# Turning the normalised rows of two of four batches with transposing DMA transfers instead of TensorE

## The chip, the cores and the metric

One core of a Trainium2 chip runs the whole kernel. The metric is the device time of one execution in microseconds (us); the profiler's span, from the first to the last instruction, is a little shorter. The core has five engines, each with its own in-order instruction stream: PE (TensorE, matrix products; PEld are its weight loads), DVE (VectorE), ACT (ScalarE), POOL (GpSimd) and SP (SyncE, which here only issues DMA transfers). Sixteen DMA engines move the data.

## The reference, cut to what matters

The input is four batches of eight heads with 768 positions of 64 values. First comes a block-sparse causal attention, then a Fourier mixing over positions and features, a normalisation of each row, and an MLP of two matrices with a residual:

```
x   = attention(q, k, v)            # per head: own block and the top 3 of 12 blocks of 64 keys
u   = x + real(fft(fft(x, axis=positions), axis=features))
un  = (u - mean(u)) / sqrt(var(u) + 1e-6)        # per row of 512
out = u + max(un @ w_ch1, 0) @ w_ch2             # 512 -> 2048 -> 512
```

The product `un @ w_ch1` contracts over the 512 features. TensorE contracts over partitions, so `un`, which is computed with positions on the partitions, has to be turned: features onto the partitions.

## The kernel before, in words

All operations of the kernel are first collected as a plan, then put in order by a planner in the kernel (class `Plan`): each operation has a rank, the engines that could do it with a cost on each, the values that it reads and writes, and PSUM banks that it holds. The planner (a list scheduler, `schedule`) starts whatever is ready first, by rank among equals, and its order is written out as the order of instructions on each engine. For a DMA operation it counts an issue cost on SP, a duration on a simulated queue, 1.9 us, and 2.5 us (`LANDING`) until a reader may start. The costs only set the order; on the chip, the engines wait for each other by semaphores.

- `attention(p)` does a pair of heads, 16 pairs in all, four to a batch. Loads of q, k and v come by SP (L367), are cast and split on POOL (casts at the helper's line L688, `klo` L466, `qhl` L461), turned on PE (L478, L527), gated (L542, L581, L585, L594, L606, L616), then scores (PE L639), exponentials (ACT L650), the causal select on the diagonal (POOL L656), the product with v (PE L668, which needs v cast to f16) and the division (DVE L677, L680). The loads of pair p are due well before the pair: their buffers are those of pair p - 2.
- `fourier(b)` does the mixing of batch b after its last pair: sums (L700, L721), two stages of products (PE L739, L743, L773), `u` (DVE L779), row statistics (L786, L789, ACT L797, L801, DVE L805) and the normalised rows, written in place into the tile `x` (`apply`: ACT L813 or DVE L817). A row tile `st` is 128 positions by 512 features, f16; six make a batch. They are done in two halves of three.
- The turn, also in `fourier(b)`: for each row tile, four TensorE transposes of 128 by 128 into one PSUM bank (`un_turn`, L831) and one copy into `unT[:, :, 128*st : 128*st+128]` on DVE (L688) or ACT (L687). There is one `unT` for all batches, [128, 4, 768] f16, so a turn must wait until the last product of the batch before has read the part that it overwrites.
- `mlp(b)` does, for each half (384 positions), 16 up-projections of four matmuls (PE L853, which read `unT` and `w_ch1`), the ReLU (ACT L865 or DVE L867), then three down-projections of 16 matmuls (PE L878), the sum with `u` (DVE L884) and a store of 256 KB to the output (SP, L367). It has a low rank, so its matmuls fill PE between the attention groups of the next batch. The MLP of batch 3, and what is left of batch 2's, run after the attention.

SP's queue thus holds the loads of q, k and v and the stores of the output, in the planner's order.

Of the kernel before, what the change touches and what calls it, by code (L numbers as in the profile page):

```python
# [278 lines left out]
def kernel(  # L279
# [9 lines left out]
    nc = tc.nc  # L289
    B, H, _, D = q.shape  # L290
# [11 lines left out]
    def sb(shape, dtype, name):  # L302
        return cpool.tile(shape, dtype, tag=name, name=name)
# [46 lines left out]
    unT = sb([128, 4, S], F16, "unT")  # L350
# [12 lines left out]
    P = Plan()  # L363
# [10 lines left out]
    def small(rank, e, cost, fn, r=(), w=(), ps=(), pre=(), port=False, rel=0.0):  # L374
        engs = e if isinstance(e, dict) else {e: cost}
        P.op(rank, engs, fn, r=r, w=w, ps=ps, pre=pre, port=port, rel=rel)
# [6 lines left out]
    for i in range(2):  # L383
        small(0.2 + i, "DVE", 0.06,
              lambda x, n, i=i: nc.vector.memset(ind32[64 * i:64 * i + 64, i:i + 1], 1.0),
              r=["ind32"], w=["ind32"])
# [6 lines left out]
    for i in range(NH):  # L393
        small(0, "DVE", 0.07, lambda x, n, i=i: nc.vector.memset(qhl[i][:, :, 0, 64:128], 0.0),
              w=[("qz", i)])
    for i in range(2):
        small(0.5, "DVE", 0.2, lambda x, n, i=i: nc.vector.memset(gmp[i], 0.0), w=[("gmp", i)])
    for i in range(NV):
        small(0.6, "DVE", 0.07, lambda x, n, i=i: nc.vector.memset(V16[i][:, :, :, 64:66], 0.0),
              w=[("vone", i)])  # L400
        small(0.6, "DVE", 0.07, lambda x, n, i=i: nc.vector.memset(V16[i][:, :, :, 64:65], 1.0),
              r=[("vone", i)], w=[("vone", i)])
# [282 lines left out]
    def _copy(x, dst, src):  # L685
        if x == "ACT":
            return nc.scalar.copy(out=dst, in_=src)  # L687
        return eng[x].tensor_copy(out=dst, in_=src)  # L688


    def fourier(b):
        base = 1000 * (HP * b + HP - 1) + (1700 if b == 0 else 500)
        x3, u2 = b % 3, b % 2
        X, U = xb[x3], ub[u2]
        fe = {"DVE": 0.27, "POOL": 0.87}
        for hp in range(HP):
            cols = slice(128 * hp, 128 * hp + 128)
            for r, op in ((0, OP.add), (1, OP.subtract)):
                small(base, fe, 0,
                      lambda x, n, cols=cols, r=r, op=op: eng[x].tensor_tensor(  # L700
                          out=fs[:, r, :, cols], in0=X[:, 0:3, cols], in1=X[:, 3:6, cols], op=op),
                      port=True,
                      r=[("x", x3, 2 * hp), ("x", x3, 2 * hp + 1)], w=[("fs", hp, r)],
# [5 lines left out]
        for i, op in ((0, OP.add), (1, OP.subtract)):  # L709
            small(base + 1, f1, 0,  # L710
                  lambda x, n, i=i, op=op: eng[x].tensor_tensor(
                      out=pm[:, i, :, 1:256], in0=fsf[:, :, 1:256], in1=fsf[:, :, 511:256:-1],
                      op=op),
                  r=allf, w=[("pm", i)], port=True)
        small(base + 1, "ACT", 0.2,
              lambda x, n: nc.scalar.copy(out=pm[:, 0, :, 0:257:256], in_=fsf[:, :, 0:257:256]),
              r=allf, w=["pm0"])
        for i, src, op, lo in ((0, 0, OP.add, 0), (1, 0, OP.subtract, 0),
                               (2, 1, OP.subtract, 0), (3, 1, OP.add, 1)):
            small(base + 2, f2, 0,  # L720
                  lambda x, n, i=i, src=src, op=op, lo=lo: eng[x].tensor_tensor(  # L721
                      out=fk[:, :, i, lo:128], in0=pm[:, src, :, lo:128],
                      in1=pm[:, src, :, 256 - lo:128:-1], op=op),
                  r=[("pm", 0), ("pm", 1), "pm0", "pmz"], w=[("fk", i)], port=True)
        small(base + 2, "ACT", 0.2,
              lambda x, n: nc.scalar.copy(out=fk[:, :, 3, 0:1], in_=pm[:, 1, :, 128:129]),
              r=[("pm", 1)], w=["fk3z"])
        small(base + 2, "ACT", 0.2,
              lambda x, n: nc.scalar.copy(out=xm[:, :, 0:1], in_=pm[:, 0, :, 128:129]),
              r=[("pm", 0)], w=["xm"])  # L730
        for i in range(4):
# [3 lines left out]
            def stage1(x, n, i=i, yp=yp, tab=tab):  # L735
                o = bank32[yp.bank][:, 0:2 * KM].rearrange("p (r m) -> p r m", r=2)
                for r in range(2):
# [3 lines left out]
                    if i == 2:  # L741
# [4 lines left out]
                 r=[("fk", i), "fk3z", "cs", "ss"] + (["xm"] if i == 2 else []),  # L746
                 w=[yp], ps=[yp], pre=[("ty", i), ("trv", i)])
            small(base + 3, {"ACT": 0.46, "DVE": 0.5}, 0,
                  lambda x, n, i=i, yp=yp: _copy(
                      x, ty[i].rearrange("p m r -> p r m"),  # L750
                      bank32[yp.bank][:, 0:2 * KM].rearrange("p (r m) -> p r m", r=2)),
                  r=[yp], w=[("ty", i)], ps=[yp])
            small(base + 3, {"ACT": 0.46, "DVE": 0.5}, 0,
                  lambda x, n, i=i, yp=yp: _copy(
                      x, tr[i].rearrange("p m r -> p r m"),
                      bank32[yp.bank][:, 1:2 * KM - 1]
                      .rearrange("p (r m) -> p r m", r=2)[:, :, ::-1]),
                  r=[yp], w=[("trv", i)], ps=[yp])
# [3 lines left out]
        for kt in range(NST):  # L762
            mp = P.psum("mm")
            late = 0 if kt < 3 else LATE

            def stage2(x, n, kt=kt, mp=mp):
                for par in range(2):
                    o = bank32[mp.bank][:, 256 * par:256 * par + 256]
                    for j in range(2):
# [7 lines left out]
                 w=[mp], ps=[mp], pre=[("u", u2, kt)])  # L777
            small(base + late + 4, "DVE", 0.61,
                  lambda x, n, kt=kt, mp=mp: nc.vector.tensor_tensor(  # L779
                      out=U[:, kt, :].rearrange("p (l r) -> p r l", r=2),  # L780
                      in0=bank32[mp.bank].rearrange("p (r l) -> p r l", r=2),
                      in1=X[:, kt, :].rearrange("p (l r) -> p r l", r=2), op=OP.add),
                  r=[mp] + xall, w=[("u", u2, kt)], ps=[mp])

            small(base + late + 5, "DVE", 0.6,
                  lambda x, n, kt=kt: nc.vector.bn_stats(out=bst[kt], in_=U[:, kt, :]),  # L786
                  r=[("u", u2, kt)], w=[("bst", kt)])
            small(base + late + 5, "DVE", 0.1,
                  lambda x, n, kt=kt: nc.vector.bn_aggr(out=stat[u2][:, kt, :], in_=bst[kt]),  # L789
                  r=[("bst", kt)], w=[("st", u2, kt)])  # L790
        for hf in range(2):
            sl = slice(3 * hf, 3 * hf + 3)
            late = LATE * hf

            vr, rs, nm = lnv[u2][:, sl], rstd[u2][:, sl], nmr[u2][:, sl]
            small(base + late + 6, "ACT", 0.2,
                  lambda x, n, vr=vr, sl=sl: nc.scalar.activation(  # L797
                      out=vr, in_=stat[u2][:, sl, 1], func=AF.Ln, bias=eps),
                  r=[("st", u2, 3 * hf + i) for i in range(3)] + ["eps"], w=[("lnv", u2, hf)])
            small(base + late + 6, "ACT", 0.2,  # L800
                  lambda x, n, vr=vr, rs=rs: nc.scalar.activation(out=rs, in_=vr, func=AF.Exp,  # L801
                                                                  scale=-0.5),
                  r=[("lnv", u2, hf)], w=[("rs", u2, hf)])
            small(base + late + 6, "DVE", 0.1,
                  lambda x, n, sl=sl, rs=rs, nm=nm: nc.vector.scalar_tensor_tensor(  # L805
                      out=nm, in0=stat[u2][:, sl, 0], scalar=-1.0, in1=rs, op0=OP.mult,
                      op1=OP.mult),
                  r=[("rs", u2, hf)] + [("st", u2, 3 * hf + i) for i in range(3)],
                  w=[("nm", u2, hf)], port=True)
            for st in range(3 * hf, 3 * hf + 3):  # L810
                def apply(x, n, st=st):
                    if x == "ACT":
                        return nc.scalar.activation(out=X[:, st, :], in_=U[:, st, :],  # L813
                                                    func=AF.Identity,
                                                    scale=rstd[u2][:, st:st + 1],
                                                    bias=nmr[u2][:, st:st + 1])
                    return nc.vector.tensor_scalar(out=X[:, st, :], in0=U[:, st, :],  # L817
                                                   scalar1=stat[u2][:, st, 0:1],
                                                   scalar2=rstd[u2][:, st:st + 1],
                                                   op0=OP.subtract, op1=OP.mult)  # L820
                small(base + late + 6, {"DVE": 0.47, "ACT": 0.6}, 0, apply,
                      r=[("u", u2, st), ("rs", u2, hf), ("nm", u2, hf)],
                      w=[("x", x3, h) for h in range(H)] if st == NST - 1 else [("un", x3, st)],
                      port=True)
                if st == NST - 1:
                    P.last_w[("un", x3, st)] = len(P.ops) - 1
                tp = P.psum("tr")

                def un_turn(x, n, st=st, tp=tp):
                    for dt in range(4):  # L830
                        nc.tensor.transpose(bank16[tp.bank][:, 128 * dt:128 * dt + 128],  # L831
                                            X[:, st, 128 * dt:128 * dt + 128], id16)
                P.op(base + late + 7, {"PE": 0.25}, un_turn, r=["sm", ("un", x3, st)], w=[tp], ps=[tp],
                     pre=[("unT", st)])
                small(base + late + 7, {"DVE": 0.34, "ACT": 0.52}, 0,
                      lambda x, n, st=st, tp=tp: _copy(
                          x, unT[:, :, 128 * st:128 * st + 128],
                          bank16[tp.bank][:, 0:512].rearrange("p (a c) -> p a c", a=4)),
                      r=[tp], w=[("unT", st)], ps=[tp])
# [50 lines left out]
    for p in range(NPAIR):  # L890
# [17 lines left out]
        if p > HP and p % HP == 1:  # L908
            fourier(p // HP - 1)
            mlp(p // HP - 1)  # L910
    fourier(B - 1)
    mlp(B - 1)

# [38 lines left out]
```

## Time and profile before

| what | us |
|---|---|
| median of three runs (313.51 to 314.13) | 313.94 |
| the profiled execution | 313.72 |
| its span | 311.5 |
| PE busy / DVE / ACT / POOL | 301.3 / 195.3 / 189.1 / 130.3 |

In the page and the answers of the trace, L12 is line 12 of the kernel. A row of groups has: line, engine, operation, output<-inputs, shapes, count, then busy time in us and the mean of one in ns, then the idle time of the engine just before, with what ended it. A row of the order of time has: start in us, length in us, engine, line, operation, output<-inputs, count, and in brackets the idle time before it. SPq is SP's queue of DMA issues; the time of such a row is the time that the issue held SP. A row of waits has: who waited, for whom, us in total, times, the longest. A matmul's length is that of one in a pipelined array: several are in flight at once.

### The profile page before, as it was taken

How to read it: one execution, taken by the hardware profiler on the slowest of the kernel's cores; microseconds unless marked ns; L12 is line 12 of the kernel's file. 1: busy time of each engine (PE TensorE's matmuls, PEld its weight loads, DVE VectorE, ACT ScalarE, POOL GpSimd, SP SyncE). 2: the span in 40 equal slices, each digit the busy share in tenths (PEclk: the TensorE clock that was granted, in tenths of full speed). 3: DMA queues.
4: the chain of work that ended last, by engine and by line, in shares of the span. 5: the costliest groups of instructions: out<-in, count | busy, mean ns of one | idle time of the engine just before them, and what ended most of it. 6: DMA issues, size and time to landing. Idle time of an engine off the chain costs nothing.

```text
span 311.5 us, 8060 instructions
## 1 busy us (share of the span) xinstructions
PE 301.3 (97%) x3097; PEld 198.5 (64%) x3097; DVE 195.3 (63%) x652; ACT 189.1 (61%) x418; POOL 130.3 (42%) x251
## 2 busy tenths in 40 slices
PE   7999999999999999999999999999999999999994
PEld 4767676766647776666666876757655865554641
DVE  4797989997655899755548797856425694002001
ACT  2579898779508788478644699708661671540710
POOL 4258897836546181748273453837025000000000
PEclk9999999999999999999999999999999999999999
DMA  8999999990066351009320760010001001101001
GB/s 218 257 241 238 246 232 217 228 189 22 0 153 176 81 121 32 36 37 237 78 61 34 187 154 1 36 36 35 2 36 67 2 1 67 37 0 67 36 34 67
DMA packets 82085, 31.12 MB, mean 100 GB/s; under 512 B 75272, under 2 KB 77492, under 8 KB 82048
## 3 DMA queue, kind: packets, MB, share of 16 engines
q1 hardware_dynamic: 77584, 25.77, 33.7%
q0 software_dynamic: 3536, 4.56, 8.1%
q8 instruction: 24, 0.39, 0.5%
q10 hardware_dynamic: 928, 0.30, 0.4%
q14 instruction: 13, 0.11, 0.1%
HBM read 28.52 MB, written 6.29 MB: 112 GB/s over the span
## 4 chain that ended last, share of the span: by engine, by line
PE 80%; DVE 9%; ACT 6%; issue 1%; DMA 1%; SPq 0%; DVEq 0%; ACTq 0%
PE bank L878 27%; PE bank L853 26%; PE bank L639 9%; PE bank L668 5%; ACT pt L650 4%; PE bank L527 3%; PE bank L739 2%; DVE u L779 2%; PE bank L773 2%; PE bank L478 2%; PE bank L831 1%; DMA kn<-in_k_dram 1%; DVE bst L786 1%; DVE qg L616 1%; PE bank L492 1%
## 5 line engine op out<-in xcount | busy, mean ns | idle before, releaser
L650 ACT ACTIVATE pt<-bank 128x512 f16<-128x512 f32 x192 | 88.3, 579 | 23.4 <-PE bank L639 21.7
L853 PE MATMUL bank<-unT,w 128*128 128x384 f16 x512 | 90.7, 326 | 0.2 <-DVE unT L688 0.2
L878 PE MATMUL bank<-w,hT 128*128 128x512 f16 x384 | 89.1, 379 | 0.0
L865 ACT ACTIVATE hT<-bank 128x384 f16<-128x384 f32 x115 | 56.3, 497 | 46.4 <-PE bank L853 45.6
L853 PEld LDWEIGHTS <-w 128*128 128x128 f16 x512 | 48.2, 98 | 30.0 <-issue 0.8
L878 PEld LDWEIGHTS <-hT 128*128 128x128 f16 x384 | 36.0, 98 | 37.6
L639 PE MATMUL bank<-qg,ki 76*128 76x128 f16 (+3 forms) x384 | 51.2, 259 | 0.7 <-ACT pt L650 0.4
L884 DVE TENSOR_TENSOR u<-bank,u 128x512 f32<-128x512 f32 x24 | 16.5, 688 | 51.1 <-PE bank L878 51.0
L639 PEld LDWEIGHTS <-ki 76*128 76x128 f16 x384 | 29.2, 97 | 10.6 <-issue 0.6
L656 POOL TENSOR_SCALAR_AFFINE_SELECT pt<-pt 128x512 f16<-128x512 f16 (+1 forms) x44 | 22.0, 522 | 25.3 <-ACT pt L650 20.6
L668 PEld LDWEIGHTS <-pt 128*128 128x128 f16 x672 | 23.8, 97 | 6.5 <-ACT pt L650 3.0
L668 PE MATMUL bank<-v,pt 128*128 128x65 f16 x672 | 25.6, 193 | 0.6 <-ACT pt L650 0.3
L616 DVE TENSOR_SCALAR qg<-bank 12x384 f16<-12x384 f16 x64 | 20.6, 322 | 7.6 <-PE bank L606 5.7
L466 POOL TENSOR_TENSOR klo<-kn,k 128x384 f16<-128x384 f32 x24 | 21.9, 913 | 5.3 <-DVE rcp L677 1.9
L461 POOL TENSOR_TENSOR qhl<-qn,qhl 128x320 f16<-128x320 f32 x26 | 20.6, 792 | 6.2 <-DVE qhl L688 4.8
L688 POOL CAST k<-kn 128x384 f16<-128x384 f32 x24 | 12.2, 507 | 19.2 <-DVE fs L721 9.0
L688 DVE COPY ki<-bank 64x768 f16<-64x768 f16 x23 | 12.7, 554 | 9.6 <-PE bank L478 7.0
L680 DVE TENSOR_TENSOR x<-bank,rcp 128x384 f16<-128x384 f32 x32 | 17.8, 555 | 0.6
L677 DVE RECIPROCAL rcp<-bank 128x6 f32<-128x6 f32 x32 | 6.2, 193 | 18.0 <-PE bank L668 10.6
L527 PE MATMUL bank<-sm,qhl 128*128 128x128 f16 x192 | 17.1, 229 | 0.1
L779 DVE TENSOR_TENSOR u<-bank,x 128x512 f32<-128x512 f32 x24 | 15.3, 681 | 1.9 <-PE bank L773 1.9
L594 POOL MEMSET gmp<- 64x5 f16 x40 | 4.6, 114 | 27.9 <-DVE gmp L585 26.8
(106 smaller groups left out, 405.6 us busy)
## 6 DMA issues: line engine op xcount, KB each, us to landing
out_dram<-u SPq DMA_DIRECT2D x24, 256.0 KB, 2.0
kn<-in_k_dram SPq DMA_DIRECT2D x28, 192.0 KB, 3.4
vn<-in_v_dram SPq DMA_DIRECT2D x28, 192.0 KB, 3.8
qn<-in_q_dram SPq DMA_DIRECT2D x26, 192.0 KB, 4.4
w<-in_moe_w_ch_dram POOLq DMA_DIRECT2D x16, 256.0 KB, 6.7
hT<-in_k_dram SPq DMA_DIRECT2D x4, 192.0 KB, 4.3
hT<-in_q_dram SPq DMA_DIRECT2D x4, 192.0 KB, 4.2
hT<-in_v_dram SPq DMA_DIRECT2D x4, 192.0 KB, 3.7
```

The lines of the kernel that those rows point to most:

```text
L466: lambda x, n, kh=kh, kl=kl, e=e: eng[x].tensor_tensor(out=kl, in0=kn[a][:, :, e, :], in1=kh, op=OP.subtract),
L527: nc.tensor.transpose(bank16[tq.bank][:, 128 * st:128 * st + 128], qhl[h2][:, e, st, :], id16)
L616: nc.vector.tensor_scalar(out=rows[:, i::2, :], in0=turned[at:at + NB, 0:3 - i, :], scalar1=-NEG, scalar2=NEG, op0=OP.mult, op1=OP.add)
L639: nc.tensor.matmul(bank32[sp.bank][:, co:co + a1 - a0], KI[e][g3][0:76, 128 * jt:128 * jt + 128], QG[e][g3][0:76, a0:a1], start=not added, ...
L650: lambda x, n, sp=sp, pt=pt, at=at, wid=wid: nc.scalar.activation(out=pt[:, at:at + wid], in_=bank32[sp.bank][:, 0:wid], func=AF.Exp, scal ...
L656: lambda x, n, pt=pt, at=at, nd=nd: nc.gpsimd.affine_select(out=pt[:, at:at + 128 * nd].rearrange("p (a c) -> p a c", a=nd), in_=pt[:, at: ...
L668: nc.tensor.matmul(o[:, st, 0:65], pt[:, col:col + 128], V16[v4][:, e, jt, 0:65], start=(i == 0), stop=(i == 20))
L688: return eng[x].tensor_copy(out=dst, in_=src)
L779: lambda x, n, kt=kt, mp=mp: nc.vector.tensor_tensor(out=U[:, kt, :].rearrange("p (l r) -> p r l", r=2), in0=bank32[mp.bank].rearrange("p ...
L853: nc.tensor.matmul(bank32[hp_.bank][:, 0:384], w1[:, dt, 128 * it:128 * it + 128], unT[:, dt, 384 * hf:384 * hf + 384], start=(dt == 0), s ...
L865: nc.scalar.activation(out=o, in_=i_, func=AF.Relu)
L878: nc.tensor.matmul(bank32[cp.bank], hT[hf][:, it, 128 * j:128 * j + 128], w2[:, it, :], start=(it == 0), stop=(it == NIT - 1))
```

## The change

In `fourier(b)`, for batches 1 and 2, the turn becomes one transposing DMA transfer for each row tile, issued from SP, which reads the f16 rows from `x` and writes `unT` directly; there is no PSUM bank, no transpose on PE and no copy. In the plan it costs SP 0.6 and the queue 1.0. Batches 0 and 3 keep the turn on PE.

```diff
                 if st == NST - 1:
                     P.last_w[("un", x3, st)] = len(P.ops) - 1
+                if 0 < b < B - 1:
+                    P.op(base + late + 7, {"SP": 0.6},
+                         lambda x, n, st=st: nc.sync.dma_start_transpose(
+                             out=unT[:, :, 128 * st:128 * st + 128], in_=X[:, st, :]),
+                         r=[("un", x3, st)], w=[("unT", st)], dma=1.0)
+                    continue
                 tp = P.psum("tr")
```

The planner makes a new order from it. Up to the first turn of batch 1 the order of PE's instructions is the same; from there on it differs in places. On SP, the three transfers of batch 1's first half stand ahead of the loads of pair 11, those of batch 2's first half ahead of the loads of pair 15 (the last pairs of batches 2 and 3); the three of each second half stand among stores of the output. Lines behind the inserted ones move by 6: L831 becomes L837, L853 L859, L878 L884.

## The prediction

> **What bounds the kernel now.** I began with the page: busy times, the chain of work that ended last, the DMA queues.
>
> ```profile
> span 311.5 us, 8060 instructions
> PE 301.3 (97%) x3097; PEld 198.5 (64%) x3097; DVE 195.3 (63%) x652; ACT 189.1 (61%) x418; POOL 130.3 (42%) x251
> PE 80%; DVE 9%; ACT 6%; issue 1%; DMA 1%; SPq 0%; DVEq 0%; ACTq 0%
> q1 hardware_dynamic: 77584, 25.77, 33.7%
> out_dram<-u SPq DMA_DIRECT2D x24, 256.0 KB, 2.0
> vn<-in_v_dram SPq DMA_DIRECT2D x28, 192.0 KB, 3.8
> ```
>
> TensorE is busy for 97% of the span and makes up 80% of the chain. But that is an average, so I cut the span into stages (time, busy time by engine, granted clock, DMA share, GB/s) and asked what PE waited for from 80 to 300 us.
>
> ```profile
> 80.00:220.00 140.00, 139.21 (x1522) 94.29 (x1520) 98.59 (x323) 90.20 (x199) 71.44 (x149) 1.00 0.33 83
> 220.00:300.00 80.00, 80.00 (x527) 46.25 (x525) 28.48 (x72) 38.38 (x82) 6.43 (x10) 1.00 0.08 30
> PE bank L639 <- ACT pt L650: 0.4, 1, 0.4
> PE bank L773 <- ACT pt L650: 0.3, 1, 0.3
> 188.44 0.38 PE L639 MATMUL bank<-qg,ki 76*128 76x128 f16 x3 [0.44 <-ACT pt L650]
> ```
>
> From 80 to 220 us, where batches 1 and 2 are turned, PE stands idle for 140.00 - 139.21 = 0.79 us; from 220 to 300 us not at all. DVE, ACT and POOL are busy for 98.59, 90.20 and 71.44 of 140 us and hold PE up only in the two short waits on ACT. The granted clock is 1.00. So from 80 us to the end the time is the sum of PE's work: an instruction taken from PE shortens the run by the time it holds PE, as long as nothing that PE then reads comes late. Work taken from DVE or ACT shortens nothing by itself.
>
> **What the change removes.** A turn of one row tile is four TensorE transposes (L831) and one copy out of PSUM (L687 on ACT or L688 on DVE). The change leaves batches 0 and 3 alone and takes 2 x 6 turns: 48 of the 96 transposes. Busy time overlaps in the pipelined array, so I take the step from the first transpose of a group to the next work in PE's order of time.
>
> ```profile
> L831 PE MATMUL bank<-sm,x x96: 216/219/230, 65.9 to 259.6; 128*128 128x128 f16 x96
> 126.36 0.83 PE L831 MATMUL bank<-sm,x 128*128 128x128 f16 x12
> 127.03 1.03 PE L878 MATMUL bank<-w,hT 128*128 128x512 f16 x4
> 194.93 0.61 PE L831 MATMUL bank<-sm,x 128*128 128x128 f16 x8
> 195.37 1.03 PE L878 MATMUL bank<-w,hT 128*128 128x512 f16 x4
> L688 DVE COPY unT<-bank 128x512 f16<-128x512 f16 x16 | 6.3, 418 | 0.6 <-PE bank L831 0.4
> L687 ACT COPY unT<-bank 128x512 f16<-128x512 f16 x8 | 4.7, 582 | 5.1 <-PE bank L831 5.0
> ```
>
> One transpose is listed with 219 ns, but twelve hold PE for 127.03 - 126.36 = 0.67 us and eight for 195.37 - 194.93 = 0.44 us: 55.5 ns each. So 48 x 55.5 ns = 2.66 us leave PE, all of it in the stage where PE has no gaps. The weight loads go with the transposes and are inside that step. The 12 copies (418 or 582 ns, 5 to 7 us together) leave engines that are not the bound; I cost them at nothing. At best, the two waits on ACT shrink with them, and then at most 0.79 us more is gained.
>
> **What it adds.** Twelve transposing transfers on SP, SBUF to SBUF, 128 KB each. The trace of before has no such transfer, so its duration must be bounded. I call t the time by which one of them pushes back whatever is behind it on SP's queue, by holding the sequencer or by filling the rings. Nearest rows, the SP queue (start, time held) around the first turns of batches 1 and 2:
>
> ```profile
> 111.79 0.37 SPq L367 DMA_DIRECT2D kn<-in_k_dram  x1
> 112.21 0.54 SPq L367 DMA_DIRECT2D qn<-in_q_dram  x1
> 114.42 1.13 SPq L367 DMA_DIRECT2D vn<-in_v_dram  x2
> 126.89 0.36 SPq L367 DMA_DIRECT2D out_dram<-u  x1
> 182.40 1.23 SPq L367 DMA_DIRECT2D vn<-in_v_dram  x2
> ```
>
> A plain store of twice the bytes holds SP for 0.36 us and has landed after 2.0 us; that is the lower end. For the upper end: the compiled instruction moves blocks of 16 rows by 128 columns, so a destination partition receives runs of 16 values, 32 bytes, and a transfer has 128 x 4 x 8 = 4096 such runs. Queue q1 spent 33.7% of 16 engines x 311.5 us on 77584 packets, 21.6 ns a packet. If each run cost as much, a transfer would take 4096 / 16 x 21.6 ns = 5.5 us. Between 0.36 and 5.5 us I take about 1 us, near the load rows (0.54 and 1.13 / 2 = 0.57 us) with something added for the smaller blocks.
>
> The Trainium skill has a rule for each end. DMA: Bandwidth & Descriptors, section Latency and other measured facts, gives a transposing DMA 261 GB/s; as an estimate that is 0.5 us of moving for 128 KB, and the sum stays 311.1. The same page, section Specifications, says that transfers under 512 B are not at line rate because the engine reads, modifies and writes; were the 32-byte runs handled so, the estimate would go to the upper end, and the sum to the slower rival below. No run here shows either.
>
> **Does PE wait for the turned rows?** In batch 1, a transfer can start when its normalised rows are written and the last up-projections of batch 0 have read the old ones; in batch 2, when the rows are written.
>
> ```profile
> 118.48 2.11 PE L853 MATMUL bank<-unT,w 128*128 128x384 f16 x12
> 119.33 0.81 ACT L813 ACTIVATE x<-u,nmr,rstd 128x512 f16<-128x512 f32 x1 [0.19 <-DVE nmr L805]
> 120.22 0.54 DVE L817 TENSOR_SCALAR x<-u,stat,rstd 128x512 f16<-128x512 f32 x1
> 120.20 0.80 ACT L813 ACTIVATE x<-u,nmr,rstd 128x512 f16<-128x512 f32 x1
> 185.69 2.21 ACT L813 ACTIVATE x<-u,nmr,rstd 128x512 f16<-128x512 f32 x3
> 134.85 0.20 PE L514 MATMUL bank<-ka,sm 128*128 128x24 f16 x2
> 137.80 0.81 PE L853 MATMUL bank<-unT,w 128*128 128x384 f16 x4
> 169.66 1.46 PE L853 MATMUL bank<-unT,w 128*128 128x384 f16 x8
> 203.95 0.20 PE L514 MATMUL bank<-ka,sm 128*128 128x24 f16 x2
> ```
>
> The first three transfers of batch 1 start at about 118.48 + 2.11 = 120.6 us, and the third has landed at 120.6 + 3t + 2.0 = 122.6 + 3t. Before, the first up-projection ran at 137.80; in the changed program's order it stands right behind the group that is at 134.85 here. With t = 1 the rows are there at 125.6, 9 us early; PE would wait only from t = 4.1. In batch 2 the first three start at 186.5 (a third of the 2.21 us after 185.69), and the first reader stands behind the group that is at 203.95 here. The second half of batch 1, turned from 126.36 on, is not read before 169.66. So the longer way from rows to rows turned costs nothing; that cover is gone only with t above 4.
>
> **What is queued behind them.** SP works in order. In the changed order the three transfers stand ahead of the loads k, q, k, q, v of pair 11 (batch 1) and of pair 15 (batch 2); before, SP ran ahead and had issued these by 114.42 + 1.13 = 115.6 and by 182.40 + 1.23 = 183.6. Now they leave after the transfers. The second half of v stands also behind an output store, which waits for DVE, and transfers four to six stand among stores. Who is hurt first is POOL, which casts v in order:
>
> ```profile
> 130.05 0.91 POOL L466 TENSOR_TENSOR klo<-kn,k 128x384 f16<-128x384 f32 x1
> 132.47 0.99 POOL L656 TENSOR_SCALAR_AFFINE_SELECT pt<-pt 128x512 f16<-128x512 f16 x2 [1.51 <-ACT pt L650]
> 133.41 0.95 POOL L688 CAST v<-vn 128x384 f16<-128x384 f32 x2
> 201.64 0.95 POOL L688 CAST v<-vn 128x384 f16<-128x384 f32 x2
> ```
>
> In batch 1 the changed order puts the first cast of v before the two selects, right behind klo, so at 130.96. The load of v is issued at 120.6 + 3t + 2.0 (four loads of 0.37 to 0.54 us with their gaps) and lands 3.8 us later, at 126.4 + 3t: 129.4 with t = 1, in time. POOL waits from t = 1.5; PE only when the selects are late, which have 1.51 us of idle time before them, so from t = 2.0. In batch 2 v lands at 186.5 + 3t + 2.0 + 3.8 = 192.3 + 3t and is wanted at about 201: from t = 2.9. With t = 1 both are hidden.
>
> **Sum.** The profiled execution took 313.72 us, 2.2 us more than its span. 313.72 - 2.66 + 0 = 311.06, so 311.1. The median of the three runs, 313.94, lies 0.2 above the profiled one; I work from the latter and leave the 0.2 to the range.
>
> **Rivals.**
> Loads pushed back (slower). Price for PE: in batch 1, 3t - 6.1 above t = 2.0 (132.5 is where the selects run, less 126.4); in batch 2, 3t - 8.7 above t = 2.9. The first alone eats the gain of 2.66 at t = 2.9, so slower begins there. At t = 4 it is 5.9 + 3.3 - 2.66 = 6.5 us, 320.3; at the upper bound of 5.5 us, 10.4 + 7.8 - 2.66 = 15.5 us, 329.3. For it: the 32-byte runs, and the cast of v that moved ahead of the selects. Against it: POOL is idle for half of this stage, and DMA is busy for 0.33 of it.
>
> Gain partly eaten: t between 2.0 and 2.9, or one wait of about 1.5 us where the new order no longer has a transpose to put between attention's groups while ACT is late: 313.72 - 2.66 + 1.5 = 312.6. For it: the 0.44 us wait on ACT at 188.44 stands right beside the turns of batch 2. Against it: ACT loses copies in the same stretch. Up to a loss of 2 to 3 us this ends within 0.2%.
>
> More gain: the 0.79 us of gaps closes too, 313.72 - 2.66 - 0.79 = 310.3. For it: DVE and ACT lose 5 to 7 us. Against it: the order fills these gaps only by chance.
>
> That the transposes of batches 1 and 2 remain can be left out: the compiled program has 48 fewer.
>
> **How the numbers follow.** Forecast 311.1 (310.6 to 311.9): 0.64. More gain, 310.3: 0.06. Partly eaten, 312.6: 0.16, of which 0.06 end within 0.2% (0.6 us, about what a measurement of this kernel can tell from no change: 313.1 to 314.3). Slower, 314.4 to 329: 0.14. So faster is 0.64 + 0.06 + 0.10 = 0.80, same 0.06, slower 0.14. The range 310.2 to 313.4 leaves out the slower rival and little else; t's upper end has its weight there and is beyond the range.
>
> **What would show it.** Right: 48 fewer transposes on PE, PE still at 139 of 140 us in the stage, the same work from 220 us on some 2.7 us earlier, transposing transfers on SP that hold it for about 1 us and have landed some 10 us before the first L853 of their batch (859 in the changed file). Wrong: a wait of POOL's cast of v on a DMA near 131 us, PE waiting for a select or for an attention group behind it, loads landing in much more than 3.8 us beside the transfers, or PE's gaps between 115 and 205 us growing past 0.79 us. The prediction is wrong outright if t is above 2.9 us, or if PE takes up the removed 2.66 us in waits on ACT.

## The result and the profile after

Over 20 runs of each, the changed kernel takes a median of 311.6 us (310.04 to 315.5) and the kernel before 314.05 us (313.19 to 317.55). The ratio is 0.9922, 95% interval [0.99, 0.9943]: 2.45 us faster (1.8 to 3.1).

The execution of the changed kernel that was profiled is not a typical one: 314.68 us, with a span of 313.0. Its page, and the row of its DMA issues for the transfers (count, median us to landing):

```profile
span 313.0 us, 7986 instructions
PE 300.1 (96%) x3049; PEld 197.3 (63%) x3049; DVE 193.8 (62%) x646; ACT 187.1 (60%) x414; POOL 127.7 (41%) x249
PE 74%; DVE 8%; DMA 6%; ACT 4%; SPq 3%; POOL 2%; issue 2%; DVEq 0%; POOLq 0%
q1 hardware_dynamic: 84112, 27.34, 36.6%
```

```profile
unT<-x SPq DMA_TRANSPOSE x12, 2.5
```

PE has 48 matmuls fewer, as it should, yet the span is longer and DMA has come into the chain. The order of time shows where:

```profile
49.42 1.12 POOL L688 CAST qhl<-qn 128x384 f16<-128x384 f32 x1 [2.69 <-DMA qn<-in_q_dram]
```

```profile
55.91 0.45 PE L527 MATMUL bank<-sm,qhl 128*128 128x128 f16 x5 [1.83 <-POOL qhl L461]
```

At 49 us POOL waits 2.69 us for a load of q, and PE 1.83 us behind it. That is about 70 us before the first instruction that the change touches: the start, whose instructions are the same in both kernels, scatters from execution to execution by several us (in this one the granted clock up to the first up-projection was 0.98 against 1.00, and PE stood idle for 7.83 us against 5.38), so traces are compared here from a mark behind it. I took the stretch from the first up-projection (L853, after the change L859) to the first down-projection after the last up-projection. Rows of the view by stages (stretch, its length, busy time and instructions of PE, PEld, DVE, ACT, POOL, clock, DMA share, GB/s), for the kernel before, for the changed one, and for a second profile of the changed one (experiment 10):

```profile
67.35:296.90 229.55, 228.76 (x2162) 147.84 (x2163) 137.69 (x429) 138.55 (x304) 85.38 (x175) 1.00 0.24 64
```

```profile
71.10:298.65 227.55, 226.34 (x2114) 145.28 (x2115) 135.56 (x423) 136.28 (x300) 81.36 (x173) 1.00 0.28 69
```

```profile
70.30:297.85 227.55, 226.34 (x2114) 145.25 (x2115) 135.58 (x423) 136.38 (x300) 81.53 (x173) 1.00 0.30 72
```

The mark stands at 67.35 us in one execution and at 71.10 in the other; from there on, the changed kernel needs 227.55 us instead of 229.55, and it repeats to 0.01 us. So the change is worth 2.00 us in this stretch (2.42 of PE's busy time less, 229.55 - 228.76 = 0.79 us of gaps become 227.55 - 226.34 = 1.21). The tail behind it is 14.60 us before and 14.35 after, but 14.35 to 14.57 in the other runs, with and without the change.

That leaves a part of the 2.45 us. A run lasts a little longer than its span, and this remainder is not the same in both kernels: 313.72 - 311.5 = 2.2 us before, 314.68 - 313.0 = 1.7 us after. It repeats: the medians over the runs are 2.2 to 2.3 us for the kernel before, 1.7 us for the changed one, 1.7 to 1.9 us for every version below with transposing transfers and 2.05 to 2.3 us for every version without. So of the 2.45 us, 2.00 come from the stretch and, by these medians, about 0.5 us from outside the span, where no instruction of the program is; what the scattering start adds or takes cannot be told from one trace each. No experiment was made on that part, and its cause stays open.

PE's waits in the changed kernel from 80 us on, and where the longest stands:

```profile
PE bank L639 <- DVE qg L616: 0.6, 1, 0.6
PE bank L773 <- ACT pt L650: 0.3, 1, 0.3
PE bank L639 <- DVE u L779: 0.2, 1, 0.2
```

```profile
189.25 0.60 PE L639 MATMUL bank<-qg,ki 76*128 76x128 f16 x4 [0.63 <-DVE qg L616]
190.05 0.38 PE L639 MATMUL bank<-qg,ki 76*128 76x512 f16 x1 [0.16 <-DVE u L779]
```

The wait of 0.44 us on ACT at 188.44 is gone; two waits on DVE, 0.79 us together, stand near its place. None is on a transfer. The transfers themselves, on SP's queue, with the summary of their line:

```profile
123.91 3.91 SPq L829 DMA_TRANSPOSE unT<-x  x3
127.91 0.54 SPq L367 DMA_DIRECT2D kn<-in_k_dram  x1
130.26 0.53 SPq L367 DMA_DIRECT2D vn<-in_v_dram  x1
190.94 4.49 SPq L829 DMA_TRANSPOSE unT<-x  x3
195.52 0.53 SPq L367 DMA_DIRECT2D kn<-in_k_dram  x1
```

```profile
L829 SPq DMA_TRANSPOSE unT<-x x12: 1195/1220/1900, 123.9 to 202.8; - x12
DMA to landing us min/median/max: 2.4/2.5/4.2
```

One transfer holds SP for 1.22 us in the median and has landed 2.5 us after its issue. Three of them push the loads back by 127.91 - 123.91 = 4.0 us in batch 1 and by 195.52 - 190.94 = 4.6 us in batch 2, so t is 1.3 and 1.5 us. What stood behind them came just in time:

```profile
133.96 0.92 POOL L466 TENSOR_TENSOR klo<-kn,k 128x384 f16<-128x384 f32 x1
134.82 0.50 POOL L688 CAST v<-vn 128x384 f16<-128x384 f32 x1
136.60 0.99 POOL L656 TENSOR_SCALAR_AFFINE_SELECT pt<-pt 128x512 f16<-128x512 f16 x2 [1.27 <-ACT pt L650]
```

```profile
139.03 0.81 PE L859 MATMUL bank<-unT,w 128*128 128x384 f16 x4
```

The cast of v follows `klo` without a wait, the select still waits for ACT, not for POOL, and the first up-projection comes at 139.03, some 10 us after the third transfer has landed (issued by 126.7, plus 2.5).

### The profile page after: what moved, and what is told of

Read it like the earlier page. It is cut to its first block, busy times and chain, and to the rows that moved or that the text cites. A ratio compares the mean times of both kernels' runs of the same rounds, so it can differ in the third digit from the quotient of the medians.

```text
span 313.0 us, 7986 instructions
## 1 busy us (share of the span) xinstructions
PE 300.1 (96%) x3049; PEld 197.3 (63%) x3049; DVE 193.8 (62%) x646; ACT 187.1 (60%) x414; POOL 127.7 (41%) x249
## 3 DMA queue, kind: packets, MB, share of 16 engines
q1 hardware_dynamic: 84112, 27.34, 36.6%
## 4 chain that ended last, share of the span: by engine, by line
PE 74%; DVE 8%; DMA 6%; ACT 4%; SPq 3%; POOL 2%; issue 2%; DVEq 0%; POOLq 0%
PE bank L884 27%; PE bank L859 26%; PE bank L639 7%; DMA qn<-in_q_dram 5%; PE bank L668 4%; SPq L367 3%; ACT pt L650 3%; PE bank L739 3%; DVE u L779 3%; PE bank L527 2%; DVE bst L786 2%; PE bank L773 1%; DMA vn<-in_v_dram 1%; PE bank L478 1%; PE bank L743 1%
## 5 line engine op out<-in xcount | busy, mean ns | idle before, releaser
L859 PE MATMUL bank<-unT,w 128*128 128x384 f16 x512 | 90.4, 326 | 0.2 <-DVE unT L688 0.2
L884 PE MATMUL bank<-w,hT 128*128 128x512 f16 x384 | 88.7, 379 | 0.0
L871 ACT ACTIVATE hT<-bank 128x384 f16<-128x384 f32 x118 | 57.7, 495 | 42.6 <-PE bank L859 40.5
L859 PEld LDWEIGHTS <-w 128*128 128x128 f16 x512 | 48.2, 98 | 30.1 <-issue 0.9
L884 PEld LDWEIGHTS <-hT 128*128 128x128 f16 x384 | 36.1, 98 | 38.1
L639 PE MATMUL bank<-qg,ki 76*128 76x128 f16 (+3 forms) x384 | 51.1, 259 | 0.9 <-DVE qg L616 0.6
L639 PEld LDWEIGHTS <-ki 76*128 76x128 f16 x384 | 29.2, 97 | 11.1 <-issue 0.9
L668 PEld LDWEIGHTS <-pt 128*128 128x128 f16 x672 | 23.8, 97 | 5.6 <-ACT pt L650 2.3
L668 PE MATMUL bank<-v,pt 128*128 128x65 f16 x672 | 25.6, 193 | 0.2
L461 POOL TENSOR_TENSOR qhl<-qn,qhl 128x320 f16<-128x320 f32 x26 | 21.3, 819 | 6.6 <-DVE qhl L688 5.2
L688 DVE COPY qg<-bank 128x768 f16<-128x768 f16 x24 | 13.2, 551 | 5.1 <-PE bank L527 3.3
```

The lines of the kernel that those rows point to most:

```text
L461: lambda x, n, hi=hi, lo=lo, e=e: eng[x].tensor_tensor(out=lo, in0=qn[a][:, e, 1:NST], in1=hi[:, 1:NST], op=OP.subtract),
L639: nc.tensor.matmul(bank32[sp.bank][:, co:co + a1 - a0], KI[e][g3][0:76, 128 * jt:128 * jt + 128], QG[e][g3][0:76, a0:a1], start=not added, ...
L668: nc.tensor.matmul(o[:, st, 0:65], pt[:, col:col + 128], V16[v4][:, e, jt, 0:65], start=(i == 0), stop=(i == 20))
L859: nc.tensor.matmul(bank32[hp_.bank][:, 0:384], w1[:, dt, 128 * it:128 * it + 128], unT[:, dt, 384 * hf:384 * hf + 384], start=(dt == 0), s ...
L871: nc.scalar.activation(out=o, in_=i_, func=AF.Relu)
L884: nc.tensor.matmul(bank32[cp.bank], hT[hf][:, it, 128 * j:128 * j + 128], w2[:, it, :], start=(it == 0), stop=(it == NIT - 1))
```

## The experiments

Theory A: the gain is PE's time, 48 transposes of 55.5 ns; copies and transfers count for nothing. Rivals: the copies (C), transfers that hold back the loads (B), and, as results came in, waits that the transposes had been covering, and the planner's new order. Each is judged by the row of the stretch defined above; where a ratio is given, it is the ratio of run times to the kernel before, on the same chip. The ratios hold the start and the time outside the span as well, so they do not measure the stretch (experiment 3's says 3.7 us where the stretch says 2.1). Diffs are against the changed kernel, where nothing else is said, and lines that only declare an unused tile are left out of them.

**1. The transfers left out, everything else in the same order.**

```diff
-                         lambda x, n, st=st: nc.sync.dma_start_transpose(
-                             out=unT[:, :, 128 * st:128 * st + 128], in_=X[:, st, :]),
+                         lambda x, n: None,
```

> The changed kernel with the twelve transposing transfers left out and every other instruction in the same order (batches 1 and 2 then multiply rows left in unT by batch 0, so its output is not the reference's). Theory A (PE's time is what was gained, the transfers are hidden): within 0.4 us of the changed kernel's 311.6. Rival B (the transfers hold back loads behind them and cost part of the gain): faster than the changed kernel by the cost, 0.5 to 1.2 us, since PE's gaps of about 1.2 us from 80 us on could go.

```profile
69.91:297.47 227.56, 226.35 (x2114) 145.29 (x2115) 135.62 (x423) 136.26 (x300) 81.36 (x173) 1.00 0.24 63
```

227.56 us with no transfer at all, 227.55 with twelve: they cost nothing in the stretch. Ratio 0.9915 [0.9881, 0.995]. B falls. The run's median, 312.38 us, is not within the expected 0.4 us of 311.6; 0.35 us of this is time outside the span (2.05 us here, 1.70 in the changed kernel), and none of it is in the stretch.

**2. The transposes put back, their result unused.**

```diff
+                    tp = P.psum("tr")
+
+                    def again(x, n, st=st, tp=tp):
+                        for dt in range(4):
+                            nc.tensor.transpose(bank16[tp.bank][:, 128 * dt:128 * dt + 128],
+                                                X[:, st, 128 * dt:128 * dt + 128], id16)
+                    P.op(base + late + 7, {"PE": 0.25}, again, r=["sm", ("un", x3, st)],
+                         w=[tp], ps=[tp])
                     continue
```

> The changed kernel with the 48 TensorE transposes put back, their result unused; the transfers still do the turning and the 12 copies stay away. Theory A (48 x 55.5 ns = 2.66 us of PE are the whole gain): the gain is gone, 314.0 to 314.4, ratio to before 1.000 +- 0.002. Rival C (the relief of DVE and ACT by 12 copies, or fewer waits for a copy): stays near 311.6, ratio 0.992.

```profile
67.01:295.95 228.94, 228.59 (x2162) 147.78 (x2163) 137.36 (x426) 136.86 (x298) 80.40 (x172) 1.00 0.30 73
```

PE's busy time comes back (228.59), but the stretch is 228.94, not 229.55; ratio 0.9937 [0.9901, 0.9974]. PE's gaps are only 0.35 us here. Neither theory had that: 0.61 us of gain is there with all the transposes in place. What else differs from the kernel before is the copies, the transfers, and the planner's order. Experiments 1 and 8 exclude the first two. The order is one of its own: apart from the transposes, PE's matmuls stand neither as in the kernel before nor as in the changed kernel.

**3. Copies added to the changed kernel**, 12 of 128 x 512 on DVE (8) and ACT (4), from SBUF to an unused tile.

```diff
+                    small(base + late + 7, {"DVE": 0.34, "ACT": 0.52}, 0,
+                          lambda x, n, st=st: _copy(
+                              x, idle[:, :, 128 * (st % 3):128 * (st % 3) + 128],
+                              U[:, st, :].rearrange("p (a c) -> p a c", a=4)),
+                          r=[("u", u2, st), ("un", x3, st)], w=[("idle", st % 3)])
```

> The changed kernel with 12 copies of 128 x 512 values added on DVE or ACT (from u in SBUF to an unused tile; those out of PSUM cannot be kept without the transposes); no transposes on PE. Theory A: within 0.4 us of 311.6, ratio 0.992, as DVE and ACT have room. Rival C (copies were the gain): back toward 314, ratio 1.000.

```profile
66.34:293.81 227.47, 226.26 (x2115) 145.26 (x2116) 137.18 (x430) 139.36 (x305) 82.70 (x173) 1.00 0.29 72
```

DVE and ACT are 1.6 and 3.1 us busier than in the changed kernel, the stretch is the same. Ratio 0.9881 [0.983, 0.9932]. Here too the planner moved some of PE's matmuls, so this is copies and a slightly different order together; experiment 8 is the one that leaves the order alone.

**8. The kernel before in its own order, the copies of batches 1 and 2 left out.**

Against the kernel before:

```diff
-                      lambda x, n, st=st, tp=tp: _copy(
+                      lambda x, n, st=st, tp=tp: None if 0 < b < B - 1 else _copy(
```

> The kernel before, its order of instructions unchanged, with the 12 copies out of PSUM of batches 1 and 2 left out (its output is not the reference's): transposes stay on PE. Theory A: 229.5 +- 0.3 us from the first up-projection to the first down-projection after the last, as before, where the changed kernel has 227.6. Rival C (the copies' relief is part of the gain): down to 228.5 or less.

```profile
70.22:299.76 229.54, 228.75 (x2162) 147.77 (x2163) 135.30 (x421) 136.30 (x300) 85.31 (x175) 1.00 0.24 63
```

229.54 against 229.55. Ratio 0.9992 [0.9958, 1.0025]. C falls: with the transposes in place, the copies are worth nothing.

**9. The kernel before in its own order, the 48 transposes left out, the copies kept.**

Against the kernel before (shown in part; the 12 copies now go from the same banks to an unused tile, `idle`):

```diff
-                    for dt in range(4):
+                    for dt in range(0 if 0 < b < B - 1 else 4):
```

> The kernel before, its order of instructions unchanged, with the 48 TensorE transposes of batches 1 and 2 left out and the 12 copies kept (as 16-bit integers from the same banks into an unused tile; batches 1 and 2 then multiply rows left by batch 0, so its output is not the reference's). Theory A (48 x 55.5 ns = 2.66 us of PE, gaps as before): 229.55 - 2.66 = 226.9 us +- 0.15 from the first up-projection to the first down-projection after the last. Rival I (a transpose between other matmuls holds PE for less than the step of a group; the changed kernel lost 2.42 us of busy time, 50 ns each): 227.1 to 227.2. Rival C (the copies): 229.5.

```profile
67.64:295.75 228.11, 226.76 (x2115) 145.18 (x2116) 137.36 (x429) 138.30 (x304) 85.55 (x175) 1.00 0.25 65
```

A miss for every theory: 228.11, only 1.44 us less than before. Ratio 0.9976 [0.9941, 1.0011]. As the order is the same, the two traces can be laid beside each other. The table gives starts on PE, and e9 less before, less the 0.29 us by which e9's mark is later (67.64 - 67.35):

| PE, what starts | before | e9 | ahead by |
|---|---|---|---|
| attention (L668) behind 8 removed transposes | 121.74 | 121.57 | 0.46 |
| k turned (L478) behind 16 more | 127.89 | 126.82 | 1.36 |
| masks turned (L606) | 129.42 | 128.62 | 1.09 |
| scores (L639) behind 8 more | 188.44 | 187.65 | 1.08 |
| scores (L639) behind 4 and 8 more | 196.24 | 194.93 | 1.60 |
| down-projection (L878) behind 4 more | 198.51 | 197.04 | 1.76 |
| attention (L668) | 200.03 | 198.88 | 1.44 |

In batch 1 the 24 transposes give 1.36 us, their full 24 x 55.5 ns = 1.33. Then part of it is given back, at the larger places before an instruction that needs another engine: 0.27 us at the turn of the masks, 0.45 us at the scores at 188 (8 transposes gone, nothing gained), 0.21 us in smaller pieces up to 198 (16 gone, 0.68 us gained instead of 0.89), 0.32 us from there to 200: 1.25 us in all, and 2.66 + 0.03 - 1.25 = 1.44. Two such places in experiment 9:

```profile
128.02 0.50 PE L529 MATMUL bank<-sm,qhl 128*128 128x128 f16 x6
128.62 0.34 PE L608 MATMUL bank<-sm,gmp 128*128 128x128 f16 x3
187.65 0.38 PE L641 MATMUL bank<-qg,ki 76*128 76x128 f16 x3 [0.89 <-ACT pt L652]
126.98 0.74 DVE L690 COPY idle<-bank 128x512 int16<-128x512 int16 x2
127.64 0.29 DVE L587 TENSOR_TENSOR gmp<-gsb,mx 128x120 f16<-128x120 f32 x1
127.99 0.57 POOL L596 MEMSET gmp<- 64x5 f16 x4 [0.20 <-DVE gmp L587]
```

The wait on ACT at 188 is 0.89 us instead of 0.44: the transposes had covered half of it. At 128 there is no wait in brackets, yet six transposes that step 55.5 ns each end their steps at 128.35 and the next matmul starts at 128.62. Of these 0.27 us, 0.17 hide under the listed length of the last matmul in flight (128.02 + 0.50 = 128.52) and count as busy; the other 0.10 is idle time too short for the view's brackets. The next matmul reads the masks `gmp`, which POOL has finished at 127.99 + 0.57 = 128.56, behind DVE. And right before that step of DVE stand two of the kept copies, 0.74 us. The changed kernel has no such copies, so up to 0.27 us of what experiment 9 gives back may be theirs; a run of the old order without transposes and without copies was not made.

**4. Every transfer issued twice, the first into an unused tile.**

```diff
-                         lambda x, n, st=st: nc.sync.dma_start_transpose(
-                             out=unT[:, :, 128 * st:128 * st + 128], in_=X[:, st, :]),
+                         lambda x, n, st=st: [nc.sync.dma_start_transpose(
+                             out=o[:, :, 128 * i:128 * i + 128], in_=X[:, st, :])
+                             for o, i in ((idle, st % 3), (unT, st))][-1],
```

> Each of the twelve transfers issued twice, the first into an unused tile. SP is then held for 2.4 us a row tile instead of 1.2. Theory A with the prediction's own price for loads pushed back (3t - 6.1 in batch 1 above t = 2.0, nothing in batch 2): 3 x 2.44 - 6.1 = 1.2 us lost, 312.8, ratio 0.996. Rival D (POOL's delay never reaches PE): 311.6, ratio 0.992. Rival E (PE pays all of the push, 3 x 1.22 us for each of two batches): 318.9, ratio 1.016.

```profile
66.77:294.33 227.56, 226.35 (x2114) 145.25 (x2115) 135.60 (x423) 136.26 (x300) 81.56 (x173) 1.00 0.33 79
```

```profile
134.04 0.50 POOL L689 CAST v<-vn 128x384 f16<-128x384 f32 x1 [3.48 <-DMA vn<-in_v_dram]
119.58 1.30 SPq L830 DMA_TRANSPOSE idle<-x  x1
127.51 0.53 SPq L368 DMA_DIRECT2D kn<-in_k_dram  x1
```

POOL now waits 3.48 us for v, and PE no longer than in the changed kernel: 227.56. Ratio 0.9877 [0.9829, 0.9925]. Rival D is right; the prediction's price, 1.2 us by the expected t of 2.44, is wrong here. By this trace t was (127.51 - 119.58) / 3 = 2.6, for which the price would be 1.8 us.

**5. Every transfer issued four times**, three into an unused tile. Against experiment 4:

```diff
-                             for o, i in ((idle, st % 3), (unT, st))][-1],
+                             for o, i in ((idle, 0), (idle, 1), (idle, 2), (unT, st))][-1],
```

> Each of the twelve transfers issued four times, three into an unused tile: SP is held for some 4.9 us a row tile. The prediction's price, 3t - 6.1 in batch 1 and 3t - 8.7 in batch 2, gives 8.6 + 6.0 = 14.6 us lost, 326, ratio 1.039. Rival F (with double transfers POOL waited 3.5 us for v and PE not at all, so PE has more slack behind the selects than the prediction counted, about 3 us more in each batch): 6 to 10 us lost, 318 to 322, with PE waiting behind POOL's selects or casts.

```profile
69.72:311.85 242.13, 229.60 (x2115) 146.61 (x2116) 135.75 (x423) 136.61 (x300) 81.67 (x173) 0.98 0.38 86
```

```profile
PE bank L669 <- POOL pt L657: 4.7, 1, 4.7
PE bank L607 <- POOL gmp L595: 4.1, 2, 2.5
PE bank L861 <- DMA unT<-x: 2.6, 1, 2.6
122.53 3.92 SPq L830 DMA_TRANSPOSE idle<-x  x3
139.11 0.58 SPq L368 DMA_DIRECT2D kn<-in_k_dram  x1
```

242.13, so 14.6 us more than the changed kernel: the expected size to the tenth, against F. That is luck. The 14.6 expected belong to t = 4.9; by the trace t was (139.11 - 122.53) / 3 = 5.5 in batch 1 and 6.0 in batch 2, for which the same formula gives 10.5 + 9.2 = 19.7 us. And the places are not the ones that it added up: 4.7 us are the attention behind POOL's select in batch 1, which it priced at 10.5; 2.6 us are the up-projection waiting for the turned rows and 4.1 us POOL's later work (the memsets of `gmp`), which it did not have. These three make 11.3 us. The other 3.3 us are busy time of PE (229.60 against 226.34, for the same matmuls), in a stretch whose granted clock is 0.98 instead of 1.00. Ratio 1.0406 [1.0341, 1.047].

**6. Batch 3 turned by transfers too.**

```diff
-                if 0 < b < B - 1:
+                if 0 < b:
```

> Batch 3 is turned by transfers as well (batches 1, 2 and 3; batch 0 stays on TensorE). Batch 3's turns lie after the attention, where only the MLP of batch 2 is left to fill PE. Theory A (PE's time counts wherever PE is full): another 24 x 50 ns = 1.2 us gone, 310.4, and 1.2 us less from the first up-projection to the first down-projection after the last. Rival G (nothing covers the 2.5 us to landing there): 0 to 3 us lost against the changed kernel.

```profile
68.05:294.26 226.21, 225.00 (x2090) 143.92 (x2091) 134.16 (x419) 135.31 (x298) 81.61 (x173) 1.00 0.31 76
```

226.21, another 1.34 us less: 24 transposes at 55.8 ns, and gaps of 1.21 us as in the changed kernel. All other matmuls of PE stand in the changed kernel's order, so here the removal is seen alone. Beside batch 3's turns PE has only MLP work left, and nothing is given back. Median 310.87, ratio 0.9876 [0.9827, 0.9925]: in the stretch this version is ahead of both kernels.

**7. Batch 0 turned by transfers too.**

```diff
-                if 0 < b < B - 1:
+                if b < B - 1:
```

> Batch 0 is turned by transfers as well (batches 0, 1 and 2). Batch 0's turns lie at 60 to 80 us, where the DMA engines are full of loads and weights and little work is there to fill PE. Theory A says that PE's time counts only where PE is full, and here it is not: no gain, and a loss of 3 to 6 us through waits for the rows of batch 0, 315 to 318. Rival H (a gain of 1.2 us for each batch turned by transfers): 310.4.

```profile
76.49:298.50 222.01, 221.74 (x2056) 141.91 (x2054) 130.60 (x396) 131.32 (x289) 74.79 (x158) 1.00 0.30 74
```

The first up-projection starts at 76.49 us, where in the other eleven traces it starts between 66.34 and 71.10. The stretch is shorter (other work has moved ahead of the mark, so the rows cannot be compared), but the run is not: ratio 1.0005 [0.9968, 1.0042], the whole gain of batches 1 and 2 is gone. Theory A's lower edge, 315, was met (315.04); H is wrong. But the loss did not come as expected, through PE's waits for the rows. What stands in PE's order where batch 0 was turned, in the kernel before and here:

```profile
65.88 0.86 PE L831 MATMUL bank<-sm,x 128*128 128x128 f16 x12
65.88 3.18 PE L390 MATMUL bank<-warm 128*128 128x512 f16 x14
66.21 5.00 SPq L829 DMA_TRANSPOSE unT<-x  x3
```

L390 is filler: matmuls on a tile of zeros whose results nobody reads, which the planner puts in where its own costs leave PE idle, up to 75 us of its plan. This program has 56 of them, all others have 33. The 23 more, at a step of 0.215 us ((3.18 - 0.38) / 13), hold PE for about 5 us and count as busy. The three transfers are issued by 71.2 us and land 2.4 us after their issue, so by about 73.6; PE reaches the up-projection at 76.49, and no wait of PE for the turned rows is listed. So the price here is the gap that the planner foresaw and filled; how long PE would have waited without filler was not tried.

**10. The changed kernel again**, with no edit.

> The changed kernel once more, unchanged. Theory A: the start, the same instructions in both kernels up to the first turn of batch 1, is what scatters from one execution to the next; the stretch from the first up-projection to the first down-projection after the last is 227.55 +- 0.15 us again, ratio to before 0.992. Rival J (the scatter comes with the transfers): that stretch differs by more than 0.5 us.

Its row is above: 227.55 again. Ratio 0.9889 [0.9839, 0.9939]. J falls; the scatter lies ahead of the mark.

## Why the prediction was right, point by point

- **48 x 55.5 ns = 2.66 us leave PE.** The step is right: 1.36 us for batch 1's 24 in experiment 9, 1.34 for batch 3's in experiment 6. "All of it in the stage where PE has no gaps" is the sentence that failed in part. 0.79 us of gaps in the view by stages did not mean that PE waited for no one: waits shorter than a matmul's listed length do not show, and some transposes stood where PE would have waited. In the old order 2.66 us bring 1.44 (experiment 9). From there to the changed kernel it is 0.56 us more (228.11 to 227.55), and with the transposes in place experiment 2 is 0.61 us below the kernel before (229.55 to 228.94). Together 1.44 and 0.56 are the 2.00 us of the stretch, 0.66 less than the term predicted. The 0.61 us are the planner's order, as copies and transfers are excluded; but it is experiment 2's order and not the changed kernel's. That the 0.56 us are the order too is argued from it, and up to 0.27 us of them may be the copies. Of the 0.61 us, 0.44 are shorter gaps (0.79 to 0.35); of the 0.56 us only 0.14 are (1.35 to 1.21), the rest is inside the busy time. Which exchanges in the order do it was not tried.
- **Copies at nothing.** Right where it was tried: with the transposes in the old order (experiment 8), and added to a new order (experiment 3).
- **t about 1 us, between 0.36 and 5.5.** 1.3 and 1.5 us. The upper end was off, by its count and not by its price: queue q1 has 84112 - 77584 = 6528 packets more, 544 a transfer, not 4096. The rows are moved in pieces of about 1.57 MB / 6528 = 240 bytes on average, not 32. q1's share grew from 33.7% of 311.5 us to 36.6% of 313.0, on 16 engines: 153 us, which is 23.5 ns a packet (21.6 were assumed), or 0.8 us of all 16 engines a transfer. Of the two rules of the Trainium skill (DMA: Bandwidth & Descriptors), that of the section Latency and other measured facts, with its estimate of 0.5 us, comes nearer to these 0.8 us. The Trainium skill's other rule (same page, section Specifications), on transfers under 512 B, was applied to 32-byte runs that the queue does not show; whether the packets of 240 bytes lose by it, no run here tells.
- **PE does not wait for the rows.** Right: 10 us of room, 9 were forecast, and with four transfers for one PE does wait there (2.6 us).
- **Loads behind them.** POOL takes v with no wait at t = 1.3 (forecast: from 1.5 on). The price above that was wrong: nothing at t = 2.6 where the formula has 1.8 us, and 14.6 at t = 5.5 to 6.0 where it has 19.7, at three places, of which it had priced one. That 14.6 was also the expected number came of a t put too low; agreement in size alone would have passed for a proof.
- **More gain** did not come; the gaps grew to 1.21 us. That PE's gaps grow past 0.79 us was one of the prediction's own signs of being wrong, and it came, if only by 0.42 us; and what the prediction had 2.7 us earlier behind 220 us came 2.00 us earlier, counted from the mark. **Partly eaten** describes the sort of loss that came, an attention group that waits where a transpose had stood, though on DVE and not on ACT, and at less than half of its price (0.66 us, not 1.5).
- **Sum.** 311.1 was forecast and 311.6 measured; 2.66 us of gain and 2.45 (1.8 to 3.1). That these two lie so close is in part luck: the term of PE's time came to 2.00 us, and about 0.5 us came from outside the span, where the prediction expected no change. What stands is the mechanism, PE's time where PE is full; its size came a quarter below the forecast.

## What to carry to other kernels

An engine at 99% busy can still be held by others: work that is taken from it at a place where it would else wait is not gained, so ask of each removed piece what comes next and whether that is ready. Look also at what the busy time is: in experiment 7 filler counted as work. Moving a transposition to DMA pays where three things hold: the matrix engine is full, other work covers some 3 us from issue to landing, and the queue has room for 1.3 to 1.5 us each ahead of its loads (batches 1, 2 and 3 here; for batch 0 the planner had only filler to put there). When a planner makes a new order from a change, try the removal in the old order as well, or its luck is taken for the change's merit. And when an expected size is met, put the measured values into the formula before believing it: the 14.6 us of experiment 5 did not survive that.

## What the runs showed of the hardware that was not expected

A transposing transfer of 128 x 512 f16 from SBUF to SBUF holds SP for 1.22 us (1.20 to 1.90), over three times as long as a store of 256 KB (0.36), and adds 544 packets to the queue. Issued back to back, with the loads behind them, three push those back by 1.3 to 1.5 us each. A 128-column matmul is listed with 219 ns and steps 55.5 ns, so up to 0.16 us of waiting behind it does not show as idle time: one of experiment 9's losses is 0.27 us with no wait in the view. The time of a run outside the profiler's span was 1.7 to 1.9 us in versions with transposing transfers and 2.05 to 2.3 us in those without; why, no run here shows.
